# Four PSUM banks for a step's seven products, their sums on VectorE, relu, square and cast on ScalarE, the low part on GpSimd

## The chip, the cores and the metric

The kernel runs on one core of one Trainium2 chip. The time is device microseconds (us) of one execution; the figure quoted is the median of several runs. Engines: PE is TensorE (PEld its weight loads), DVE is VectorE, ACT is ScalarE, POOL is GpSimd, SP issues DMAs.

## What is computed

```python
X = np.fft.rfft(x, axis=1)                      # x: 8 x 3008 x 256
Yr = Xr @ w_r - Xi @ w_i + b_r
Yi = Xr @ w_i + Xi @ w_r + b_i
Y  = soft_threshold(Yr, 0.01) + 1j * soft_threshold(Yi, 0.01)
y  = np.fft.irfft(Y, n=3008, axis=1).reshape(24064, 256)
h  = y @ w_in                                   # 256 x 2048
out = (np.maximum(h, 0) ** 2) @ w_out           # 2048 x 256
```

All inputs are float32. Most products are made with numbers split in a high and a low part of type fp32r (a cast for the high part, a subtraction for the low one): high x high, high x low, low x high, three matmuls for one product.

## The kernel before

**The transform (called the first half here).** 3008 = 47 x 64, so a batch goes through four stages. `Fwd` is the 47-point part: per batch 13 pieces of 120 x 256, each loaded, folded by a sum and a difference (GpSimd), split, multiplied with `am_sb`, and stored to DRAM (`s1`). `Pair` takes two of 24 groups of bins: `fwd` (64-point part, plain float32, four matmuls), `sums` (a third operand), `mix` and `shrink` (the products with w_r and w_i, 18 matmuls, bias and soft threshold), `back` (six matmuls) and a store to `s3`. `Back` loads two rows of `s3`, splits them (`split`: ScalarE casts, GpSimd subtracts three times) and multiplies with `dx_sb` (`mm`); VectorE adds the two halves of the result into `yr`, which holds the columns of one token tile. Batch 0 goes through plain float32 twins of these (`Fwd32`, `Unit32`) in a front part, in which w_in and w_out are also unpacked from 64-bit floats.

**The second half.** The 48 token tiles (six for a batch, 500 or 504 tokens) go through 8 steps each, 384 steps in all. A step `Step(t, n)` makes 256 columns of `h` for its tile as a 2 x 2 block product with seven half-size products instead of eight (Strassen and Winograd): `Tokens.sums` and `split` make the seven operands of the tile (`yt0`, `yt1`, on GpSimd and ScalarE), `win_sums` those of w_in. Each of the seven is three matmuls of 250 or 252 columns (L474), 21 a step. `first` issues all seven into three PSUM banks `pa`, `pb`, `pc`, the last one (A12 x B21) into the half of `pa` that p1 was copied from: ScalarE copies p1, VectorE forms u2 (L488), v (L489) and the four quarters of `c` (L490, L493, L496). `second` makes relu and square: quarters 0 and 1 in one VectorE operation (L500), quarters 2 and 3 in two of ScalarE (L501, L502); then ScalarE casts all four to `mg0` and VectorE subtracts for the low part `mg1` (both in the helper `halves`, L84 and L88). `out(j)` is six matmuls of 500 or 504 columns with w_out into two accumulators `pso0` and `pso1` (L515), two `out` a step; after a tile's last step ScalarE copies the accumulators and they are stored.

**PSUM** has eight banks: two for `pso`, three in turn for the step's `psh`, three in turn for everything of the first half (`psf`).

**Order.** The program is written slot by slot: slot 2n holds `first` of step n and the second `out` of step n-2, slot 2n+1 `second` of step n and the first `out` of step n-1. The tasks of the first half for the next two batches are sorted by due slots (`pair_tasks`, `fwd_tasks`, `back_tasks`) and put between. A scheduler then sets the order of each engine's instructions, from its own estimate of times. Loads on SP's queue follow each other (`load_next`); constants for `Pair.back` (`kcm`) are loaded by GpSimd's queue. Each engine executes its instructions in the order given.

## Time and profile before

| | us |
|---|---|
| median of 3 runs | 2931.07 (2927.35 to 2939.08) |
| the profiled execution's own time | 2935.55 |
| its span, first to last instruction | 2933.8 |
| PE busy | 2681.6 (91%), 17038 matmuls |
| PEld busy | 2383.9 (81%) |
| DVE busy | 2262.4 (77%) |
| ACT busy | 1603.8 (55%) |
| POOL busy | 1696.1 (58%) |

The busy time of a pipelined matmul runs to its modelled end, while the next one has already started; so the distance between starts in the timeline tells what a matmul costs, and the idle time before a weight load tells what PE waited for. A wait for several semaphores is put down to the one that came last.

### The profile page before, as it was taken

To read this page: it belongs to the slowest core of one execution; us is meant where nothing else is said; L and a number is where in the kernel's file an instruction comes from. 1 tells how busy PE (TensorE), PEld (TensorE's weight loads), DVE (VectorE), ACT (ScalarE), POOL (GpSimd) and SP (SyncE) were. 2 spreads that over 40 slices of the span, in tenths; PEclk is the share of its full clock that TensorE was granted. 3 is DMA by queue.
4 is the path that set the end of the run, shared out by engine and by line. 5 is a ranking of instruction groups with operands and counts; after the bars stand their busy time and mean duration, and the time that the engine had idled before them with its cause. 6 is when DMAs were issued, how large, how long until landed. Compare 5 with 4: busy or idle time off the path is not lost.

```text
span 2933.8 us, 47287 instructions
## 1 busy us (share of the span) xinstructions
PE 2681.6 (91%) x17038; PEld 2383.9 (81%) x17038; DVE 2262.4 (77%) x3835; ACT 1603.8 (55%) x3147; POOL 1696.1 (58%) x1689
## 2 busy tenths in 40 slices
PE   5678988999999998999899998999999999999998
PEld 3567877888888887888788887888888888888787
DVE  5855877788888877788767887788877877877776
ACT  2455555555565565556455564556555555555554
POOL 1076776776767586576656765577766546433310
PEclk9889999999999999999999999999999999999999
DMA  8322232232222222122221221122221111100000
GB/s 238 126 62 88 84 89 72 73 87 74 74 70 80 66 82 77 42 77 82 64 63 58 74 83 56 56 69 77 79 69 51 57 47 54 42 16 28 16 15 15
DMA packets 139179, 200.35 MB, mean 68 GB/s; under 512 B 14611, under 2 KB 87683, under 8 KB 138947
## 3 DMA queue, kind: packets, MB, share of 16 engines
q1 hardware_dynamic: 126403, 174.49, 19.5%
q0 software_dynamic: 12544, 22.84, 3.3%
q8 instruction: 136, 2.23, 0.3%
q14 instruction: 96, 0.79, 0.1%
HBM read 121.91 MB, written 75.37 MB: 67 GB/s over the span
## 4 chain that ended last, share of the span: by engine, by line
PE 41%; DVE 24%; POOL 14%; ACT 7%; DMA 7%; issue 6%; SPq 0%; POOLq 0%; DVEq 0%; ACTq 0%
PE pso L515 19%; PE psh L474 13%; DVE mg L88 6%; PE psf L276 4%; POOL dul L88 3%; DMA du<-s 3%; DVE kv L298 3%; DVE mv L489 3%; DVE mc L500 2%; POOL duh L88 2%; ACT mg L84 2%; POOL yt L88 2%; POOL mc L88 2%; DVE mu L488 1%; POOL xs L204 1%
## 5 line engine op out<-in xcount | busy, mean ns | idle before, releaser
L515 PE MATMUL pso<-mg,wout 128*128 128x500 f32 (+1 forms) x4608 | 1219.1, 400 | 69.9 <-DVE mg L88 41.9
L474 PE MATMUL psh<-yt,win 128*128 128x250 f32 (+1 forms) x8064 | 1111.2, 283 | 53.4 <-DVE mu L488 28.0
L474 PEld LDWEIGHTS psh<-yt,win 128*128 128x128 f32 x8064 | 1047.3, 191 | 102.5 <-DVE mu L488 35.7
L515 PEld LDWEIGHTS pso<-mg,wout 128*128 128x128 f32 x4608 | 823.2, 191 | 248.7 <-DVE mg L88 88.6
L88 DVE TENSOR_TENSOR mg<-mc,mg 128x1000 fp32r<-128x1000 f32 (+1 forms) x384 | 549.8, 1432 | 202.4 <-ACT mg L84 201.3
L501 ACT ACTIVATE mc<-mc 128x500 f32<-128x500 f32 (+1 forms) x384 | 239.7, 624 | 414.7 <-DVE mc L493 414.0
L84 ACT CAST mg<-mc 128x1000 fp32r<-128x1000 f32 (+1 forms) x384 | 396.6, 1033 | 83.4 <-DVE mc L500 75.6
L500 DVE SCALAR_TENSOR_TENSOR mc<-mc 128x500 f32<-128x500 f32 (+1 forms) x384 | 363.5, 947 | 9.0
L489 DVE TENSOR_TENSOR mv<-psh,mu 128x500 f32<-128x500 f32 (+1 forms) x384 | 260.5, 678 | 46.4 <-PE psh L474 13.5
L88 POOL TENSOR_TENSOR duh<-du,duh 32x512 fp32r<-32x512 f32 x128 | 186.7, 1458 | 162.7 <-ACT duh L84 123.9
L493 DVE TENSOR_TENSOR mc<-psh,mv 128x500 f32<-128x500 f32 (+1 forms) x384 | 256.8, 669 | 0.7 <-PE psh L474 0.4
L488 DVE TENSOR_TENSOR mu<-psh,mp 128x250 f32<-128x250 f32 (+1 forms) x384 | 158.6, 413 | 125.1 <-ACT mp L84 123.3
L502 ACT ACTIVATE mc<-mc 128x500 f32<-128x500 f32 (+1 forms) x384 | 239.7, 624 | 7.6
L88 POOL TENSOR_TENSOR dul<-du,duh 64x256 fp32r<-64x256 f32 x256 | 227.5, 889 | 18.8
L88 POOL TENSOR_TENSOR xl<-xs,xh 120x256 fp32r<-120x256 f32 x182 | 166.0, 912 | 108.6 <-ACT xh L84 70.4
L496 DVE TENSOR_TENSOR mc<-psh,mp 128x250 f32<-128x250 f32 (+1 forms) x384 | 157.8, 411 | 89.6 <-PE psh L474 88.5
L276 PE MATMUL psf<-wx,kxh 128*128 128x256 f32 x1008 | 217.5, 286 | 5.7 <-DVE yr L436 3.1
L88 POOL TENSOR_TENSOR ksl<-kv,ksh 128x512 fp32r<-128x512 f32 x84 | 124.8, 1486 | 148.6 <-ACT ksh L84 147.1
L84 ACT COPY mp<-psh 128x250 f32<-128x250 f32 (+1 forms) x384 | 140.2, 365 | 109.0 <-PE psh L474 93.1
L88 POOL TENSOR_TENSOR mc<-yr 128x250 f32<-128x250 f32 (+1 forms) x96 | 72.0, 772 | 211.6 <-DVE mg L88 209.8
L204 POOL TENSOR_TENSOR xs<-xt 120x256 f32<-120x256 f32 x182 | 156.0, 857 | 51.8 <-DMA xt<-x_in 39.6
L276 PEld LDWEIGHTS psf<-wx,kxh 128*128 128x128 f32 x1008 | 171.4, 192 | 11.3 <-issue 2.9
(96 smaller groups left out, 3576.6 us busy)
## 6 DMA issues: line engine op xcount, KB each, us to landing
s<-ku SPq DMA_DIRECT2D x192, 128.0 KB, 1.8
du<-s SPq DMA_DIRECT2D x128, 192.0 KB, 2.7
s<-xe SPq DMA_DIRECT2D x92, 240.0 KB, 2.4
xt<-x_in SPq DMA_DIRECT2D x91, 240.0 KB, 3.2
kcm<-cm_in POOLq DMA_DIRECT2D x84, 256.0 KB, 3.3
ka<-s SPq DMA_DIRECT2D x84, 256.0 KB, 3.5
out<-mo SPq DMA_DIRECT2D x64, 250.0 KB, 2.1
kb<-bm_in SPq DMA_DIRECT2D x84, 128.0 KB, 2.1
```

Of the source, the lines that this page charges most:

```text
L84: return act.copy(out=out, in_=in_)
L88: return eng.tensor_tensor(out=out, in0=a, in1=b, op=ALU.subtract)
L204: return eng.tensor_tensor(out=out[:, :n], in0=self.xt[:, :n, 0], in1=self.xt[:, :n, 1], op=(ALU.add, ALU.subtract)[t])
L276: self.last = nc.tensor.matmul(ps, l, wx[j][:, k, c, :], start=n == 0, stop=n == 5)
L474: nc.tensor.matmul(ps, win[w][:, self.n, a], y[:, b], start=j == 0, stop=j == 2)
L488: dve.tensor_add(out=u2, in0=pa[:, 1], in1=p1)
L489: dve.tensor_tensor(out=v, in0=pb, in1=u2.unsqueeze(1).broadcast_to([128, 2, h]), op=ALU.add)
L493: dve.tensor_add(out=c[:, 1:3], in0=pc, in1=v)
L500: dve.scalar_tensor_tensor(out=c[:, 0:2], in0=c[:, 0:2], scalar=0.0, in1=c[:, 0:2], op0=ALU.max, op1=ALU.mult)
L501: act.activation(c[:, 2:4], c[:, 2:4], AF.Relu)
L502: act.activation(c[:, 2:4], c[:, 2:4], AF.Square)
L515: nc.tensor.matmul(acc[t][d][:, :2 * h], wout[w][:, f, dsl], self.g[g][:, j], start=f == 0 and k == 0, stop=f == NF - 1 and k == 2,)
```

## The change

Nine things are changed together.

1. A step has four banks of its own, one buffer each: `pa` (A11, S2), `pb` (S1, S3), `pc` (S4, A22), `pd` (A12); `psf` has two banks in the main part instead of three (six in the front part).
2. `first` issues four products, `second` the other three. p1 is copied by VectorE.
3. Relu, square and cast of all four quarters run on ScalarE as three operations of 1000 or 1008 columns; the subtraction for the low part runs on GpSimd. L500 and the VectorE subtraction are gone.
4. The slots are: 2n: `first` of n, first `out` of n-2; 2n+1: second `out` of n-2, then `second` of n.
5. `then` chains every matmul of the steps, and every operation of the steps on VectorE, ScalarE and GpSimd, in program order; the scheduler can only put work of the first half between.
6. `Fwd` is one float32 matmul each for sum and difference instead of three fp32r ones: no split, one ScalarE copy of 512 columns instead of two of 256, one bank instead of two.
7. The split of what `Back` reads is made before the store: `store_back` stores a high and a low part (two stores instead of one); the low part is a VectorE subtraction from PSUM, in the front part a GpSimd one. `Back` loads in three DMAs instead of one and multiplies at once.
8. In `Pair` the third operand is added by VectorE from PSUM and the bias likewise; two GpSimd sums, one more addition and a ScalarE copy are gone.
9. `Tokens` runs in smaller pieces (two `sums`, four `split`), `yr` has one buffer, and columns that belong to the next tile wait in `dy` and are copied by GpSimd (`put`). Due slots are new.

```diff
 MAIN = {
-    "xt": 1, "xs": 1, "xh": 1, "xl": 1, "xe": 1, "du": 1, "duh": 1, "dul": 1, "kv": 1, "kp": 1, "kq": 1, "ksh": 1,
-    "ksl": 1, "kxl": 1, "mo": 1, "mp": 1, "mu": 1, "mv": 1, "mc": 3, "kb": 1,
+    "xs": 1, "xe": 1, "du": 1, "kv": 1, "kp": 1, "kq": 1, "ksh": 1, "ksl": 1, "kxl": 1, "kb": 1, "yr": 1,
+    "ms": 1, "mp": 1, "mu": 1, "mv": 1, "mc": 3, "mo": 1,
 }
...
+        def run(self):
+            ps = bank([128, 2, D])
+            for t in range(2):
+                nc.tensor.matmul(ps[:M1, t], am32[:, t], self.u[:, t], start=True, stop=True)
+            self.ev = T("xe", [M1, 1, 2, D], F32)
+            copy(act, self.ev[:, 0], ps[:M1])
+            self.store()
+
+    def store_back(b, g, ps, eng):
+        uh = T("kuh", [128, D], F32R)
+        ul = T("kul", [128, D], F32R)
+        done = copy(act, uh, ps)
+        if eng is None:
+            sub(dve, ul, ps, uh)
+        else:
+            u = T("ku", [128, D], F32)
+            done = copy(act, u, ps)
+            sub(eng, ul, u, uh)
+        rows = s3[b].rearrange("m p c -> (m p) c")
+        for v, m in ((uh, 4 * g), (ul, 128 + 4 * g if 4 * g < 64 else 32 + 4 * g)):
+            nc.sync.dma_start(rows[m * NP:m * NP + 128], v.bitcast(F32))
+        return done
...
+    def then(eng, op, *args, **kwargs):
+        with tc.issue_after(last_of[eng].ins) if eng in last_of else nullcontext():
+            last_of[eng] = op(*args, **kwargs)
...
         def first(self):
-            pa, pb, pc = (ps_h.tile([128, 2, 256], F32, name="psh")[:, :, :h] for _ in range(3))
+            self.ps = pa, pb, pc, pd = [bank([128, 2, 256], f"psh{j}")[:, :, :h] for j in range(4)]
...
-            copy(act, p1, pa[:, 0])
-            dve.tensor_add(out=u2, in0=pa[:, 1], in1=p1)
...
+            then(dve, copy, dve, p1, pa[:, 0])
+            then(dve, dve.tensor_add, out=u2, in0=pa[:, 1], in1=p1)
+            then(dve, dve.tensor_add, out=v, in0=pb, in1=u2.unsqueeze(1).broadcast_to([128, 2, h]))
+            then(dve, dve.tensor_add, out=c[:, 3], in0=pb[:, 0], in1=v[:, 1])
+
+        def second(self):
+            h, c = self.h, self.c
+            pc, pd = self.ps[2:]
             self.product(pc[:, 0], S4, B22)
             self.product(pc[:, 1], A22, T4)
-            dve.tensor_add(out=c[:, 1:3], in0=pc, in1=v)
-
-            self.product(pa[:, 0], A12, B21)
-            dve.tensor_add(out=c[:, 0], in0=pa[:, 0], in1=p1)
-
-        def second(self):
-            h, c = self.h, self.c
-            dve.scalar_tensor_tensor(out=c[:, 0:2], in0=c[:, 0:2], scalar=0.0, in1=c[:, 0:2], op0=ALU.max, op1=ALU.mult)
-            act.activation(c[:, 2:4], c[:, 2:4], AF.Relu)
-            act.activation(c[:, 2:4], c[:, 2:4], AF.Square)
...
-            halves(self.g[0], self.g[1], c.rearrange("p (f j) h -> p f (j h)", f=2), dve)
+            self.product(pd[:, 0], A12, B21)
+            then(dve, dve.tensor_add, out=c[:, 1:3], in0=pc, in1=self.v)
+            then(dve, dve.tensor_add, out=c[:, 0], in0=pd[:, 0], in1=self.p1)
...
+            then(act, act.activation, c, c, AF.Relu)
+            then(act, act.activation, c, c, AF.Square)
+            then(act, copy, act, g[0], c)
+            then(pool, sub, pool, g[1], c, g[0])
...
         n, k = divmod(m, 2)
+        if k and 0 <= n - 2 < len(steps):
+            steps[n - 2].out(1)
         if n < len(steps):
             (steps[n].second if k else steps[n].first)()
-        if 0 <= n - 2 + k < len(steps):
-            steps[n - 2 + k].out(1 - k)
+        if not k and 0 <= n - 2 < len(steps):
+            steps[n - 2].out(0)
```

Three places show how the order moves. Names end in buffer numbers, which tie an operand to the instruction that made it; `x2` is two such instructions in a row.

PE, in the last tile, before: the last product of a step, then `out` of the step ahead of it (`mg0_33597` is made from `psh_33554`, the step before `psh_33607`).

```order
L474 MATMUL psh_33607<-yt0_33167,win0_90 128x250
L474 MATMUL psh_33607<-yt0_33167,win1_91 128x250
L474 MATMUL psh_33607<-yt1_33168,win0_90 128x250
L515 MATMUL pso0_33334<-mg0_33597,wout0_92 128x500
L515 MATMUL pso0_33334<-mg0_33597,wout1_93 128x500
L515 MATMUL pso1_33335<-mg0_33597,wout0_92 128x500
L515 MATMUL pso1_33335<-mg0_33597,wout1_93 128x500
L515 MATMUL pso0_33334<-mg1_33598,wout0_92 128x500
```

PE, the same place in the change: the fourth product of `first`, then `out` of the step two ahead (`mg0_32125` is made from `psh0_32078`; the steps `psh0_32131` and `psh0_32184` lie after it).

```order
L455 MATMUL psh1_32185<-yt0_31666,win0_81 128x250
L455 MATMUL psh1_32185<-yt0_31666,win1_82 128x250
L455 MATMUL psh1_32185<-yt1_31667,win0_81 128x250
L455 MATMUL pso0_31941<-mg0_32125,wout0_83 128x500
L455 MATMUL pso0_31941<-mg0_32125,wout1_84 128x500
L455 MATMUL pso0_31941<-mg1_32126,wout0_83 128x500
```

Between the last product of a step and the first use of its `mg1` there now stand 33 products and 14 matmuls of `out`; before there stood 21 and 16.

VectorE, one step in the last tile, before:

```order
L488 TENSOR_TENSOR mu_33611<-psh_33607,mp_33610 128x250
L489 TENSOR_TENSOR mv_33612<-psh_33608,mu_33611 128x500
L88 TENSOR_TENSOR mg1_33598<-mc_33560,mg0_33597 128x1000
L496 TENSOR_TENSOR mc_33613<-psh_33607,mp_33610 128x250
L490 TENSOR_TENSOR mc_33613<-psh_33608,mv_33612 128x250
L493 TENSOR_TENSOR mc_33613<-psh_33609,mv_33612 128x500
L500 SCALAR_TENSOR_TENSOR mc_33613<-mc_33613 128x500
```

And in the change:

```order
L89 COPY mp_32188<-psh0_32184 128x250
L455 TENSOR_TENSOR mu_32189<-psh0_32184,mp_32188 128x250
L455 TENSOR_TENSOR mv_32190<-psh1_32185,mu_32189 128x500
L455 TENSOR_TENSOR mc_32191<-psh1_32185,mv_32190 128x250
L455 TENSOR_TENSOR mc_32191<-psh2_32186,mv_32190 128x500
L455 TENSOR_TENSOR mc_32191<-psh3_32187,mp_32188 128x250
```

The two operations that read and write SBUF alone (L500 and the subtraction) are gone; the copy of p1 has come, and every operation left reads PSUM.

ScalarE in the middle of the program, two steps, before (`psf`, `kv`, `xs` are tiles of the first half):

```order
L501 ACTIVATE mc_14471<-mc_14471 128x504
L84 COPY ke_15498<-psf_15480 128x512
L502 ACTIVATE mc_14471<-mc_14471 128x504
L84 CAST mg0_14538<-mc_14471 128x1008
L84 COPY mp_14569<-psh_14566 128x252
L501 ACTIVATE mc_14572<-mc_14572 128x504
L84 CAST xh_15696<-xs_15695 120x256
L84 COPY xe_15427<-psf_15589 120x256
L502 ACTIVATE mc_14572<-mc_14572 128x504
L84 COPY mp_14687<-psh_14684 128x252
L84 CAST ksh_15579<-kv_15571 128x512
L84 CAST mg0_14624<-mc_14572 128x1008
```

ScalarE in the change, two steps in the middle of the program:

```order
L455 ACTIVATE mc_13675<-mc_13675 128x1008 x2
L88 CAST mg0_13715<-mc_13675 128x1008
L88 COPY kq_13729<-psf_13721 128x256
L88 CAST kxh_13726<-psf_13721 128x512
L455 ACTIVATE mc_13756<-mc_13756 128x1008
L88 COPY dy_13734<-psf_13735 128x188
L88 CAST kxh_13726<-kp_13728 128x256
L455 ACTIVATE mc_13756<-mc_13756 128x1008
L88 CAST ksh_13660<-kv_13652 128x512
L88 CAST mg0_13811<-mc_13756 128x1008
```

GpSimd over the same two steps in the change (before, no operation of a `Step` stood on this engine):

```order
L92 TENSOR_TENSOR mg1_13716<-mc_13675,mg0_13715 128x1008
L92 TENSOR_TENSOR kxl_13727<-kp_13728,kxh_13726 128x256
L92 TENSOR_TENSOR ms_13791<-yr_13436 128x252
L92 TENSOR_TENSOR ksl_13661<-kv_13652,ksh_13660 128x512
L92 TENSOR_TENSOR mg1_13812<-mc_13756,mg0_13811 128x1008
```

The step's three ScalarE operations stand in a fixed order with operations of the first half between them, and the subtraction for `mg1` stands among GpSimd's work of the first half.

## Rows read from the trace of the kernel before

**Rows 1.** The page, part 1: span and busy time of each engine.

```profile
span 2933.8 us, 47287 instructions
...
PE 2681.6 (91%) x17038; PEld 2383.9 (81%) x17038; DVE 2262.4 (77%) x3835; ACT 1603.8 (55%) x3147; POOL 1696.1 (58%) x1689
```

**Rows 2.** Timeline, PE, 2709 to 2714 us: start, us, engine, line, count.

```profile
2709.37 1.90 PE L474 MATMUL psh<-yt,win 128*128 128x252 f32 x15
...
2711.11 2.90 PE L515 MATMUL pso<-mg,wout 128*128 128x504 f32 x12
...
2713.84 2.27 PE L474 MATMUL psh<-yt,win 128*128 128x252 f32 x18
```

**Rows 3.** Timeline, one step near the end; in brackets idle before, and releaser.

```profile
2906.21 2.60 PE L474 MATMUL psh<-yt,win 128*128 128x250 f32 x21
...
2908.62 1.19 DVE L88 TENSOR_TENSOR mg<-mc,mg 128x1000 fp32r<-128x1000 f32 x1
...
2908.65 3.30 PE L515 MATMUL pso<-mg,wout 128*128 128x500 f32 x12
...
2909.87 1.67 PEld L515 LDWEIGHTS pso<-mg,wout 128*128 128x128 f32 x8 [0.57 <-DVE mg L88]
...
2911.79 2.60 PE L474 MATMUL psh<-yt,win 128*128 128x250 f32 x21
...
2912.95 1.03 ACT L84 CAST mg<-mc 128x1000 fp32r<-128x1000 f32 x1
...
2914.20 1.19 DVE L88 TENSOR_TENSOR mg<-mc,mg 128x1000 fp32r<-128x1000 f32 x1
```

**Rows 4.** Lines by form, PEld: busy us, mean ns, idle before (us), releasers.

```profile
L474 PEld LDWEIGHTS psh<-yt,win 128*128 128x128 f32 x8064 | 1047.3, 191 | 102.5 <-DVE mu L488 35.7 <-DVE mc L496 17.1 <-issue 6.3
...
L515 PEld LDWEIGHTS pso<-mg,wout 128*128 128x128 f32 x4608 | 823.2, 191 | 248.7 <-DVE mg L88 88.6 <-ACT mg L84 27.1 <-ACT mo L84 6.9
...
L224 PEld LDWEIGHTS psf<-xh,am_sb 120*120 120x120 f32 x364 | 59.0, 189 | 31.0 <-ACT xh L84 24.4 <-DVE yr L436 1.5 <-ACT ku L84 0.9
...
L224 PEld LDWEIGHTS psf<-xl,am_sb 120*120 120x120 f32 x182 | 33.8, 186 | 9.8 <-POOL xl L88 8.9
```

**Rows 5.** Lines by form, PE: products of `Fwd.half`, and float32 ones of `Unit32`.

```profile
L224 PE MATMUL psf<-xh,am_sb 120*120 120x256 f32 x364 | 79.1, 297 | 20.9 <-ACT xh L84 18.2 <-DVE yr L436 1.9 <-ACT ku L84 0.5
...
L224 PE MATMUL psf<-xl,am_sb 120*120 120x256 f32 x182 | 53.5, 294 | 6.4 <-POOL xl L88 6.0 <-DVE mc L493 0.3
...
L373 PE MATMUL psf<-w,kx 128*128 128x256 f32 x192 | 50.1, 407 | 1.4 <-ACT kx L366 1.0
```

**Rows 6.** Timeline near 130 us, PE, float32 products of 256 columns.

```profile
130.32 1.89 PE L373 MATMUL psf<-w,kx 128*128 128x256 f32 x8
```

**Rows 7.** Lines by form, VectorE, ScalarE, GpSimd, operations of the steps.

```profile
L88 DVE TENSOR_TENSOR mg<-mc,mg 128x1000 fp32r<-128x1000 f32 x256 | 365.2, 1427 | 121.8 <-ACT mg L84 121.2
...
L500 DVE SCALAR_TENSOR_TENSOR mc<-mc 128x500 f32<-128x500 f32 x256 | 238.1, 930 | 6.1
...
L489 DVE TENSOR_TENSOR mv<-psh,mu 128x500 f32<-128x500 f32 x256 | 173.3, 677 | 29.1 <-PE psh L474 7.1 <-DVE mu L488 1.4
...
L488 DVE TENSOR_TENSOR mu<-psh,mp 128x250 f32<-128x250 f32 x256 | 105.8, 413 | 104.9 <-ACT mp L84 103.7
...
L88 POOL TENSOR_TENSOR yt<-mc,yt 128x1000 fp32r<-128x1000 f32 x32 | 67.8, 2120 | 65.6 <-ACT yt L84 65.3
...
L88 POOL TENSOR_TENSOR yt<-mc,yt 128x1008 fp32r<-128x1008 f32 x16 | 41.3, 2579 | 20.2 <-ACT yt L84 20.0
```

**Rows 8.** Windows: us, PE, PEld, DVE, ACT, POOL busy, PEclk, DMA, GB/s.

```profile
60.00:130.00 70.00, 51.98 (x235) 42.25 (x236) 69.31 (x164) 32.98 (x81) 0.00 (x0) 0.95 0.48 152
...
300.00:2934.00 2634.00, 2465.23 (x15934) 2206.69 (x15933) 2076.28 (x3462) 1473.47 (x2858) 1571.40 (x1553) 0.98 0.21 62
```

**Rows 9.** Waits: who waited, for whom: us in total, times, longest us.

```profile
POOL ksl L88 <- ACT ksh L84: 147.1, 34, 13.8
...
ACT duh L84 <- DMA du<-s: 83.7, 53, 4.5
```

More of the change, by code (lines that the diff above doesn't have):

```diff
@@ L1 @@
-from contextlib import ExitStack
+from contextlib import ExitStack, nullcontext
 import numpy as np
@@ L510, in out @@
             if f == 0:
-                acc[t] = [ps_o.tile([128, 512], F32, name=f"pso{d}") for d in range(2)]
+                acc[t] = [bank([128, 512], f"pso{d}") for d in range(2)]
             for d in range(2):
@@ L543, in fwd_tasks @@
         for q in range(J):
-            f, at = Fwd(b, q), start + 2 * q * step
-            jobs += [(at, f.load), (at, lambda f=f: f.half(0)), (at + step, lambda f=f: f.half(1))]
+            f, at = Fwd(b, q), start + q * step
+            jobs += [(at - 2.5, f.load), (at - 0.8, f.add), (at + 0.3, f.run)]
         return jobs
```

235 lines of the change are left out of this document (118 added, 117 removed).

## The prediction, made before the changed kernel had run

> **What bounds the kernel now.** Read the page's busy times first: TensorE (PE) is busy 91% of 2933.8 us, VectorE 77%, GpSimd 58%, ScalarE 55% [rows 1]. No engine is full, so the next question is what a step costs when PE waits for nothing, and what it costs as it is. A dense piece of the timeline answers the first: 15 products take from 2709.37 to 2711.11 us, 0.116 us each, and 12 matmuls of `out` from 2711.11 to 2713.84, 0.2275 us each [rows 2]. A step is 21 and 12 of them: 2.44 + 2.73 = 5.17 us. In the last tiles, where no work of the first half is left, the steps start 5.58 us apart (2906.21 and 2911.79), so 0.41 us is lost in each, and the row in it names what for: the weight load of `out` waits for VectorE's subtraction [rows 3]. That subtraction (2908.62 to 2909.81) also stands ahead of the next step's sums, so VectorE is part of a loop that runs slower than PE.
>
> For the whole run I take the idle time ahead of the weight loads. For the products it is 102.5 us. For `out` it is 248.7 us, but a load (0.191 us) is shorter than a 0.2275 us matmul, and 4608 x 0.036 = 168 us of idle come from that alone; so I count only what has a named releaser: 88.6 + 27.1 + 6.9 = 122.6 us [rows 4]. Together the steps wait **225 us**. The two operations of VectorE that touch SBUF alone are also unsteady: the 1000-column subtraction has a mean of 1427 ns against 1.19 us in the quiet stretch [rows 3, 7], the 500-column relu and square 930 ns against 677 ns for a sum of the same width from PSUM [rows 7].
>
> **The change, part by part.** The sum is made against the profiled execution's own 2935.55 us, which is 4.5 us above the median of 2931.07.
>
> *Waits of the steps.* VectorE loses both operations that touch SBUF alone, (1427 + 930) ns a step, and gains a copy like L488's 413 ns; what is left is 4 x 0.413 + 2 x 0.677 = 3.0 us of a 5.17 us step. ScalarE has three operations of 1000 columns, priced as the cast's 1.03 us [rows 3]: 3.1 us. GpSimd has one subtraction, 2.12 us as for `yt` (2.58 at 1008 columns) [rows 7]. None of them can bound a pure step; the loop through VectorE is open. What has to fit now is the way from the last product of a step to the first use of its `mg1`. PE has 33 products and 14 matmuls of `out` to do meanwhile: 3.83 + 3.19 = 7.0 us. The way itself is the rest of the 0.68 us sum (0.33, as three products run beside it), 0.41, 3 x 1.03 and 2.12, 5.95 us (6.4 at 1008), plus four hand-overs. The longest in view is 0.22 us (cast ended 2913.98, subtraction began 2914.20 [rows 3]), and the others are shorter, so I take 0.5 us in all: 6.45 to 6.9 us. It fits by 0.1 to 0.6 us. In the stages with work of the first half the window is longer: counted in the order of instructions with the spacings above, half the steps have 9.0 us or more and one in ten under 7.7; ScalarE's other work between relu and cast adds 0.4 us in the middle case and over 1.3 in one of ten. So the 0.41 us per step go, 384 x 0.41 = 157 us, and the remaining 225 - 157 = 68 us, delays by other work in the queues, I leave standing. **-157 us**, bounds -225 (all gone) and 0 (new waits take their place); a price above zero is the second rival's.
>
> *`Fwd` in plain float32.* Removed are 546 products of 256 columns [rows 5], at the spacing above 256/252 x 0.116 = 0.118 us: 64.4 us. Added are 182 float32 matmuls, which the profile shows as two each: eight such took 1.89 us with 0.41 for the last, so 0.211 us apart [rows 5, 6]: 364 x 0.211 = 76.8. **+12 us**, on PE's own time. With the split goes what PE waited for: 31.0 + 9.8 us ahead of these loads [rows 4]. About 10 us I keep for the folds that now release PE directly: **-31 us**, bounds -41 and 0.
>
> *`Back` without a split.* The split's ScalarE cast and GpSimd subtractions go, hidden work today. But PE then waits for the load itself, and ScalarE waited 83.7 us in 53 places for it [rows 9]. The product is due 1.6 slots behind its load, where the split was due after 1.5, so a late load would show on PE. I take **0**, bounds -20 and +84. The extra DMAs (1283 issued on SP's queue for 835) lie beside a DMA share of 0.21 [rows 8].
>
> *Two `psf` banks for three.* In the order 32 of some 760 sums of the first half have less than 1.5 us of PE's work between the sum that held their bank and themselves, against 42 of some 850 before. A bank is freed by one copy behind at most a 1.03 us cast, so at worst 32 x 1.6 = 51 us. **+10 us**, bounds 0 and 51.
>
> *Clock.* From 300 us on the granted clock averages 0.98 [rows 8]; with levels of 2.4 and 1.2 GHz that costs 0.02 x 2634 = 53 us. Fewer waits should leave fewer falls, but weight loads run ahead of the matmuls, so part of the 225 us above never reached them, and I take only **-10 us**, bounds 0 and -40.
>
> *Both ends.* In the front part VectorE is busy 69.3 of 70 us [rows 8], and 24 GpSimd subtractions now run beside it. If each lengthens one of its operations as L500 is lengthened (930 - 677 ns), that is 6 us; I take +5. At the end the 6.45 us way lies behind one `out` pair (2.73) instead of a shorter way: +2. **+7 us**, bounds 0 and 15.
>
> GpSimd stays under the span even if nothing is taken off it: 1696.1 + 256 x 2.12 + 128 x 2.58 = 2569 us [rows 1, 7]. The smaller additions on VectorE and ScalarE fit in what those lose or have free.
>
> Sum: 2935.55 - 157 + 12 - 31 + 0 + 10 - 10 + 7 = 2766.5, and 4.5 less for the median: **2762 us**, 5.8% below before.
>
> **The rivals.**
>
> *1. Most waits stay.* If the waits come from the shared queues rather than the loop through VectorE, only a third of the 225 us goes, and the clock gives nothing: 2935.55 - 75 + 12 - 31 + 10 + 7 - 4.5 = 2854 us. For it: 0.1 to 0.6 us of room is thin, and a chain of three engines meets three queues. Against: the window is longer wherever the queues are fuller.
>
> *2. GpSimd holds the low part up: slower.* Its queue is in order, and today `ksl` waits there for ScalarE's `ksh` 147.1 us in 34 places, 4.3 us each [rows 9]. If each of the 84 pairs held the next `mg1` that long, with 1 us of it in the room, PE would lose 84 x 3.3 = 277 us: 2762 + 277 = 3039 us. The change loses from the point where a pair's hold takes all it saves, 169/84 = 2.0 us beyond the room, so from about 3 us. Against it: in the order shown, ScalarE's cast of `ksh` stands ahead of the very cast that `mg1` needs, so part of the hold is a wait that `mg1` has anyway. The Trainium skill (GPSIMD Engine Reference, sections 3 and 4.1) speaks against this move: elementwise work with two inputs belongs on VectorE, since GpSimd takes about twice as long. The trace agrees in direction, 2120 ns against 1427 and 1190 [rows 3, 7]; by that rule alone the outcome would be this rival.
>
> *3. Nearly dense.* If the unsteadiness of VectorE is what made the queues late, all 225 us go, the banks cost nothing and the clock gives 40: 2935.55 + 12 - 225 - 31 - 40 + 7 - 4.5 = 2654 us. For it: no step's VectorE operation is left that reads two SBUF tiles, and those from PSUM keep their 677 and 413 ns. The Trainium skill (SBUF — State Buffer, section "two separate sides") states why: VectorE with two SBUF inputs and GpSimd lock the same pair of ports against each other for a whole instruction. The 1427 and 930 ns [rows 7] agree, and by that rule the outcome leans to this rival. Against: the first half keeps its own waits, and ScalarE's queue is as mixed as before.
>
> *4. One wait for another.* The steps wait as long as before for something else, a tile's late operands or its accumulators: 2935.55 + 12 - 31 + 10 + 7 - 4.5 = 2929 us, no change.
>
> **How the numbers follow.** The forecast has 0.50, rival 1 0.20, rival 3 0.15, rival 4 0.06, rival 2 0.09. A change of 0.5%, 15 us, is about what can be told from none. Faster: 0.50 + 0.20 + 0.15 = 0.85; same 0.06; slower 0.09. The range reaches down to rival 3 (2650) and up past rival 1 with the two-bank bound added, 2854 + 41 = 2895, so 2900; outside lie rivals 2 and 4.
>
> **What would show it.** The last tiles' steps start 5.2 us apart; the waits of weight loads named after `mg` and `mu` fall from 225 to about 70 us; PE's waits for `xh` and `xl` are gone and float32 matmuls 0.21 us apart stand in their place; VectorE's step operations keep 413 and 677 ns; GpSimd's subtraction is near 2.1 us. Wrong would be: long waits of PE for GpSimd's `mg` (rival 2), for `du` loads, or for evacuations of `psf`; or last steps that still start 5.5 us apart.

## The result, and the profile after

| | before | after |
|---|---|---|
| median | 2932.42 us (4 runs, 2927.35 to 2939.08) | 2754.43 us (4 runs, 2750.85 to 2756.83) |
| profiled span | 2933.8 us | 2751.2 us |
| mean granted clock | 0.972 | 0.978 |

The change makes the kernel faster by 178 us: ratio 0.9391, 95% interval 0.9368 to 0.9413. The forecast was 2762 us. The page of the changed kernel, part 1, against [rows 1]:

```profile
span 2751.2 us, 47098 instructions
...
PE 2614.5 (95%) x16856; PEld 2362.4 (86%) x16856; DVE 1748.7 (64%) x3787; ACT 1663.6 (60%) x2434; POOL 1635.3 (59%) x1282
```

PE's busy share is 95%, VectorE's fell from 77 to 64%, and GpSimd stays below 60% although 912 us of low parts were put on it. The lines by form of PE's weight loads, as in [rows 4] (busy us, mean ns, idle before, releasers; in this kernel L455 is the line of every operation of a step, L228 the float32 products of `Fwd`, L432 the first products of `Back`):

```profile
L455 PEld LDWEIGHTS psh<-yt,win 128*128 128x128 f32 x8064 | 1035.0, 190 | 55.3 <-ACT yt L88 15.7 <-POOL yt L92 5.1
L455 PEld LDWEIGHTS pso<-mg,wout 128*128 128x128 f32 x4608 | 832.0, 190 | 170.2 <-POOL mg L92 21.7 <-ACT mo L88 7.5 <-ACT mg L88 0.7
...
L228 PEld LDWEIGHTS psf<-xs,am 120*120 120x120 f32 x364 | 57.9, 188 | 14.1 <-POOL xs L207 8.2 <-DVE yr L442 2.6
...
L432 PEld LDWEIGHTS psf<-dx_sb,du 128*128 128x128 f32 x256 | 49.5, 193 | 33.9 <-issue 20.6 <-ACT mg L88 2.9 <-DMA du<-s 2.6
```

Counted as the prediction counted, the steps wait 55.3 + 21.7 + 7.5 + 0.7 = 85 us, for 225 before [rows 4]. VectorE's u2 and `mg` are gone from the releasers. The operations of a step by form, as in [rows 7]:

```profile
L455 DVE TENSOR_TENSOR mv<-psh,mu 128x500 f32<-128x500 f32 x256 | 173.4, 678 | 24.5 <-PE psh L455 2.5 <-DVE mu L455 0.5
...
L455 DVE TENSOR_TENSOR mu<-psh,mp 128x250 f32<-128x250 f32 x256 | 106.8, 417 | 7.2
...
L89 DVE COPY mp<-psh 128x250 f32<-128x250 f32 x256 | 106.4, 415 | 32.2 <-PE psh L455 21.5
```

```profile
L92 POOL TENSOR_TENSOR mg<-mc,mg 128x1000 fp32r<-128x1000 f32 x256 | 605.2, 2364 | 394.4 <-ACT mg L88 393.6
L92 POOL TENSOR_TENSOR mg<-mc,mg 128x1008 fp32r<-128x1008 f32 x128 | 307.3, 2401 | 226.3 <-ACT mg L88 226.0
```

VectorE's sums from PSUM keep their time, 678 and 417 ns, with GpSimd at work beside them. GpSimd's subtraction takes 2364 and 2401 ns. The timeline of the last tile, where the steps run alone (PE, VectorE, ScalarE, GpSimd):

```profile
2719.59 2.62 PE L455 MATMUL psh<-yt,win 128*128 128x250 f32 x21
...
2724.81 2.61 PE L455 MATMUL psh<-yt,win 128*128 128x250 f32 x21
...
2725.71 0.68 DVE L455 TENSOR_TENSOR mc<-psh,mv 128x500 f32<-128x500 f32 x1 [1.93 <-PE psh L455]
...
2726.74 2.12 ACT L455 ACTIVATE mc<-mc 128x1000 f32<-128x1000 f32 x2 [2.00 <-DVE mc L455]
...
2728.93 1.03 ACT L88 CAST mg<-mc 128x1000 fp32r<-128x1000 f32 x1
...
2729.97 1.21 PE L455 MATMUL psh<-yt,win 128*128 128x250 f32 x9
...
2730.04 2.35 POOL L92 TENSOR_TENSOR mg<-mc,mg 128x1000 fp32r<-128x1000 f32 x1 [2.86 <-ACT mg L88]
```

The products of successive steps start 5.22 and 5.16 us apart, for 5.58 before [rows 3]. The first nine products of the 21 at 2724.81 end a step, near 2725.9; relu, square and cast follow at 2726.74 and 2728.93, and GpSimd is done at 2730.04 + 2.35 = 2732.39. That way of 6.5 us is the one that the prediction laid out (6.45 to 6.9 us, room for 7.0).

**An account of the span.** A weight load stands ahead of every matmul, so the loads' busy time and the idle time ahead of them add up to the span, less about 6 us. With the idle time split by what the load is for (sums over the groups of that view), the kernels that are compared below read, in us:

| kernel | loads busy | idle, products | idle, `out` | idle, first half | span | clock |
|---|---|---|---|---|---|---|
| before | 2383.9 | 102.5 | 248.7 | 192.7 | 2933.8 | 0.972 |
| engines and slots alone | 2407.5 | 119.5 | 166.7 | 218.2 | 2918.0 | 0.962 |
| four banks alone | 2371.7 | 85.0 | 174.7 | 204.3 | 2842.1 | 0.978 |
| after | 2362.4 | 55.3 | 170.2 | 157.1 | 2751.2 | 0.978 |
| after, no fixed order | 2349.9 | 71.0 | 123.3 | 136.2 | 2686.5 | 0.987 |
| the same, old `Back` | 2361.1 | 83.4 | 136.7 | 156.8 | 2744.1 | 0.980 |

Not all of the idle time is waiting: of the 170.2 us ahead of `out` after the change only 29.9 have a releaser among those listed above. From before to after the idle time ahead of the products gives 47 us, that ahead of `out` 78, that of the first half 36, and the loads' own time 21, together the 183 us of the span.

### The profile page after: what moved, and what is told of

It reads as the page before. It is cut to its first block, busy times and chain, and to the rows that moved or that the text cites. A ratio compares the mean times of both kernels' runs of the same rounds, so it can differ in the third digit from the quotient of the medians.

```text
span 2751.2 us, 47098 instructions
## 1 busy us (share of the span) xinstructions
PE 2614.5 (95%) x16856; PEld 2362.4 (86%) x16856; DVE 1748.7 (64%) x3787; ACT 1663.6 (60%) x2434; POOL 1635.3 (59%) x1282
## 4 chain that ended last, share of the span: by engine, by line
PE 75%; POOL 6%; DVE 5%; ACT 4%; issue 3%; DMA 2%; POOLq 0%; SPq 0%; DVEq 0%; ACTq 0%
PE pso L455 33%; PE psh L455 27%; PE psf L293 6%; POOL mg L92 2%; PE psf L228 2%; PE psf L325 2%; PE psf L272 2%; ACT mc L455 2%; DVE kv L314 1%; DVE mc L455 1%; DMA du<-s 1%; POOL xs L207 1%; POOL yt L92 1%; PE psf L436 1%; PE psf L435 1%
## 5 line engine op out<-in xcount | busy, mean ns | idle before, releaser
L92 POOL TENSOR_TENSOR mg<-mc,mg 128x1000 fp32r<-128x1000 f32 (+1 forms) x384 | 912.5, 2376 | 620.7 <-ACT mg L88 619.6
L455 PE MATMUL pso<-mg,wout 128*128 128x500 f32 (+1 forms) x4608 | 1167.3, 395 | 20.1 <-POOL mg L92 13.8
L455 PE MATMUL psh<-yt,win 128*128 128x250 f32 (+1 forms) x8064 | 1102.5, 283 | 14.3 <-ACT yt L88 12.5
L455 PEld LDWEIGHTS psh<-yt,win 128*128 128x128 f32 x8064 | 1035.0, 190 | 55.3 <-ACT yt L88 15.7
L455 ACT ACTIVATE mc<-mc 128x1000 f32<-128x1000 f32 (+1 forms) x768 | 802.6, 1045 | 374.9 <-DVE mc L455 365.5
L455 PEld LDWEIGHTS pso<-mg,wout 128*128 128x128 f32 x4608 | 832.0, 190 | 170.2 <-POOL mg L92 21.7
L455 DVE TENSOR_TENSOR mc<-psh,mv 128x500 f32<-128x500 f32 (+3 forms) x768 | 419.4, 548 | 573.3 <-PE psh L455 538.7
L455 DVE TENSOR_TENSOR mv<-psh,mu 128x500 f32<-128x500 f32 (+1 forms) x384 | 260.6, 679 | 37.5 <-PE psh L455 5.7
L89 DVE COPY mp<-psh 128x250 f32<-128x250 f32 (+1 forms) x384 | 159.7, 416 | 88.4 <-PE psh L455 72.1
L314 DVE TENSOR_TENSOR kv<-psf,ke 64x256 f32<-64x256 f32 x336 | 141.9, 422 | 58.0 <-PE psf L293 45.5
L455 DVE TENSOR_TENSOR mu<-psh,mp 128x250 f32<-128x250 f32 (+1 forms) x384 | 160.5, 418 | 11.1
L455 DVE TENSOR_TENSOR mc<-psh,mp 128x250 f32<-128x250 f32 (+1 forms) x384 | 157.3, 410 | 12.7 <-PE psh L455 10.7
L88 ACT COPY dy<-psf 128x188 f32<-128x188 f32 x256 | 76.2, 311 | 121.8 <-PE psf L436 121.4
L293 PE MATMUL psf<-wx,kxl 128*128 128x256 f32 x504 | 142.4, 283 | 2.2 <-DVE kxl L92 2.2
L88 ACT COPY xe<-psf 120x512 f32<-120x512 f32 (+1 forms) x98 | 56.8, 580 | 124.4 <-PE psf L228 104.9
L88 ACT CAST kuh<-psf 128x256 fp32r<-128x256 f32 x192 | 68.0, 373 | 98.4 <-PE psf L325 83.0
L92 POOL TENSOR_TENSOR yt<-yr,yt 128x250 fp32r<-128x250 f32 (+1 forms) x96 | 89.7, 937 | 61.8 <-ACT yt L88 61.8
```

The source lines that it names most:

```text
L88: return act.copy(out=out, in_=in_)
L89: return eng.tensor_copy(out=out, in_=in_)
L92: return eng.tensor_tensor(out=out, in0=a, in1=b, op=ALU.subtract)
L293: self.last = nc.tensor.matmul(ps, l, wx[j][:, k, c, :], start=n == 0, stop=n == 5)
L314: dve.tensor_add(out=v[64 * r:64 * r + 64, g], in0=ps[gs], in1=self.e[gs, r])
L455: last_of[eng] = op(*args, **kwargs)
```

## The experiments

All times are medians of several runs, each compared with runs of the kernel before on the same chip (its medians there: 2926 to 2931 us). The edits are against the changed kernel unless another is named.

### 1. The low part on VectorE

```diff
-            then(pool, sub, pool, g[1], c, g[0])
+            then(dve, sub, dve, g[1], c, g[0])
```

> The changed kernel, with the low part back on VectorE and all else as changed. Theory (the gain is the opened loop through VectorE: no operation of a step on it touches SBUF alone): VectorE's busy time rises by about 384 x 1.43 = 550 us to 2300, the subtraction's mean is again 1.35 to 1.45 us beside GpSimd's work, and at least half of the gain of 178 us is lost: 2840 to 2900 us. Rival (the gain is the longer room, 33 products and 14 matmuls between a step's last product and its mg1): the way to mg1 gets 1.1 us shorter (1.2 for 2.35 us), so nothing is lost: 2735 to 2770 us.

Measured: 3412.66 us, ratio 1.167 (1.1651 to 1.1689), slower than before and outside both ranges. The timeline near the end, VectorE and PE:

```profile
3351.98 0.97 PE L455 MATMUL psh<-yt,win 128*128 128x250 f32 x6 [1.36 <-DVE mu L455]
...
3357.31 1.20 DVE L92 TENSOR_TENSOR mg<-mc,mg 128x1000 fp32r<-128x1000 f32 x1 [3.24 <-ACT mg L88]
...
3359.35 0.97 PE L455 MATMUL psh<-yt,win 128*128 128x250 f32 x6 [1.29 <-DVE mu L455]
```

The subtraction itself takes 1.20 us, half of GpSimd's. But the fixed order puts it ahead of the next step's copy of p1, so VectorE stands 3.24 us for ScalarE's cast, and PE stands behind VectorE's u2. Steps start 7.37 us apart. What costs here is a place in an in-order queue, not the operation.

### 2. All old engines

p1 is copied by ScalarE, quarters 0 and 1 take one VectorE operation, the low part is on VectorE; order, banks, slots and first half as changed.

```diff
-            then(dve, copy, dve, p1, pa[:, 0])
+            then(act, copy, act, p1, pa[:, 0])
...
-            then(act, act.activation, c, c, AF.Relu)
-            then(act, act.activation, c, c, AF.Square)
+            then(
+                dve, dve.scalar_tensor_tensor, out=c[:, 0:2], in0=c[:, 0:2], scalar=0.0, in1=c[:, 0:2],
+                op0=ALU.max, op1=ALU.mult,
+            )
+            then(act, act.activation, c[:, 2:4], c[:, 2:4], AF.Relu)
+            then(act, act.activation, c[:, 2:4], c[:, 2:4], AF.Square)
...
-            then(pool, sub, pool, g[1], c, g[0])
+            then(dve, sub, dve, g[1], c, g[0])
```

> The changed kernel with all of the old engines for a step: p1 copied by ScalarE, quarters 0 and 1 by VectorE in one operation, 2 and 3 by ScalarE, low part by VectorE; order, banks and first half as changed. Theory (loop through VectorE): most of the gain of 178 us is gone, 2860 to 2930 us. Rival (room): the way is no longer than now, 2740 to 2780 us.

Measured: 2819.85 us, ratio 0.964 (0.9626 to 0.9654), between the ranges. In the fixed order the new engines are worth 65 us. PE's loads by form show where:

```profile
L455 PEld LDWEIGHTS psh<-yt,win 128*128 128x128 f32 x8064 | 1039.3, 189 | 142.5 <-DVE mu L455 51.4 <-PE psh L455 51.1 <-DVE mc L455 2.4
```

Idle time ahead of the products is 142.5 us for 55.3; 51.4 of it are put down to u2 again, and 51.1 to PE's own matmuls.

### 3. The old slots

```diff
-    for m in range(2 * len(steps) + 4):
+    for m in range(2 * len(steps) + 3):
...
-        if k and 0 <= n - 2 < len(steps):
-            steps[n - 2].out(1)
         if n < len(steps):
             (steps[n].second if k else steps[n].first)()
-        if not k and 0 <= n - 2 < len(steps):
-            steps[n - 2].out(0)
+        if 0 <= n - 2 + k < len(steps):
+            steps[n - 2 + k].out(1 - k)
```

> The changed kernel with the slots of before: second out of n-2 after first, first out of n-1 after second. Between a step's last product and the first use of its mg1 stand 21 products and 8 matmuls of out, 2.44 + 1.82 = 4.3 us, against a way of about 6.9 us. Theory and rival agree in sign. If the way is as long as worked out, PE waits 1 to 2.6 us a step: 384 x 1 to 384 x 2.6, 3130 to 3750 us. If the room does not matter (the waits of before were VectorE's unsteadiness alone): under 2820 us.

Measured: 2852.56 us, ratio 0.9753 (0.9739 to 0.9768), 98 us above the change, again between the ranges. The upper range rested on a miscount: by the slots of this run 14 matmuls of `out` (6 + 6 + 2), not 8, stand between a step's last product and its first use of `mg1`, so the room is 2.44 + 3.19 = 5.6 us against a way of 6.5. The last tiles show it; timeline of PE:

```profile
2785.55 1.21 PE L455 MATMUL psh<-yt,win 128*128 128x250 f32 x9
...
2787.41 1.18 PE L455 MATMUL pso<-mg,wout 128*128 128x500 f32 x4 [0.19 <-POOL mg L92]
...
2791.19 1.21 PE L455 MATMUL psh<-yt,win 128*128 128x250 f32 x9
```

The steps start 5.64 us apart there, about half a microsecond more than in the change; over the whole run it is 98 / 384 = 0.26 us a step. The predicted wait for the low part is there, 75.9 us for 21.7:

```profile
L455 PEld LDWEIGHTS pso<-mg,wout 128*128 128x128 f32 x4608 | 791.8, 190 | 192.8 <-POOL mg L92 75.9 <-ACT mo L88 14.5 <-ACT mg L88 9.2
```

But all idle time ahead of `out` grew by 23 us only. That of the first half grew by 86, from 157.1 to 242.9: where the scheduler has work of the first half to put between, PE's loads wait for that work's own casts and subtractions instead.

### 4. No fixed order

```diff
     def then(eng, op, *args, **kwargs):
-        with tc.issue_after(last_of[eng].ins) if eng in last_of else nullcontext():
-            last_of[eng] = op(*args, **kwargs)
+        op(*args, **kwargs)
```

> The changed kernel without the chaining of a step's instructions: the scheduler is free again to order them. Theory (engines and room): 2740 to 2790 us, no more than 1% lost. Rival (the fixed order is what pays): 2820 to 2900 us, with waits of PE for mg and yt like before.

Measured: **2688.85 us**, ratio 0.9193 (0.9179 to 0.9207), 65 us below the change and outside both ranges. PE's loads by form, then PE's timeline in the last tiles:

```profile
L454 PEld LDWEIGHTS psh<-yt,win 128*128 128x128 f32 x8064 | 1062.1, 190 | 71.0 <-ACT yt L88 6.6 <-POOL yt L92 5.5 <-issue 5.0
L454 PEld LDWEIGHTS pso<-mg,wout 128*128 128x128 f32 x4608 | 812.5, 189 | 123.3 <-POOL mg L92 4.9
```

```profile
2648.60 1.79 PE L454 MATMUL psh<-yt,win 128*128 128x250 f32 x14
2650.23 1.06 PE L454 MATMUL pso<-mg,wout 128*128 128x500 f32 x4
2651.12 0.98 PE L454 MATMUL psh<-yt,win 128*128 128x250 f32 x7
2651.94 2.02 PE L454 MATMUL pso<-mg,wout 128*128 128x500 f32 x8
2653.79 0.86 PE L454 MATMUL psh<-yt,win 128*128 128x250 f32 x6
```

`out` waits 4.9 us for GpSimd's `mg` instead of 21.7. PE takes products and `out` in pieces, here of 4 to 14, as the scheduler estimated them to be ready, where the fixed order has blocks of 9, 12 and 21. By the account, `out` stands 47 us less than in the change, the first half 21 less, the products 16 more, and the loads take 13 less. In the fixed order a late piece stops PE; the changed kernel's timeline, ScalarE and PE, shows it at a change of tiles:

```profile
2705.81 0.57 ACT L88 COPY mo<-pso 128x500 f32<-128x500 f32 x1 [3.26 <-DMA out<-mo]
...
2706.44 2.32 PE L455 MATMUL pso<-mg,wout 128*128 128x500 f32 x9 [1.04 <-ACT mo L88]
...
2712.02 2.57 PE L455 MATMUL pso<-mg,wout 128*128 128x500 f32 x10 [0.36 <-POOL mg L92]
```

ScalarE's copy of an accumulator waits 3.26 us for the DMA of the one before, the relu behind it is late, and PE stands twice, for the copy and then for `mg`.

### 5. Engines and slots on the kernel before

The edits of runs 2 and 3 made the other way on the kernel before: p1's copy, relu and square, and the low part move as in the change, and the new slots are used. Banks, first half and the scheduler's order are the old ones.

```diff
-            copy(act, p1, pa[:, 0])
+            copy(dve, p1, pa[:, 0])
...
-            halves(self.g[0], self.g[1], c.rearrange("p (f j) h -> p f (j h)", f=2), dve)
+            halves(self.g[0], self.g[1], c.rearrange("p (f j) h -> p f (j h)", f=2), pool)
```

> The kernel before with two parts of the change only: the engines (p1 copied by VectorE, relu, square and cast of all four quarters on ScalarE, low part on GpSimd) and the new slots. Three psh banks in turn, the old first half, no fixed order. Theory A (engines and slots together take the step's waits away, the banks and the first half are worth little, and the scheduler is free as in the run without the fixed order, which took 2688.85): 2690 to 2740 us. Theory B (with three banks, and all seven products issued at once, the products of the next step wait for the sums on VectorE, and the fourth bank is what lets the new slots work): 2790 to 2860 us.

Measured: 2914.86 us, ratio 0.9948 (0.9933 to 0.9963), so these two parts, on which the prediction's largest term rested, are worth 16 us alone. Both theories fall. In the account, `out` waits 82 us less, but products, first half and loads take 66 us more, and the clock falls to 0.962. The page, part 1, and PE's loads by form:

```profile
PE 2669.3 (91%) x17038; PEld 2407.5 (83%) x17038; DVE 1653.4 (57%) x3451; ACT 1804.0 (62%) x2763; POOL 2349.1 (81%) x2073
```

```profile
L309 PEld LDWEIGHTS psf<-ksh,kcm 128*128 128x128 f32 x336 | 56.4, 207 | 48.7 <-ACT ksh L84 44.7 <-issue 0.3 <-DVE yr L436 0.3
```

ScalarE and GpSimd now carry the step's work and the whole old first half, and one operand of `Pair.back`, cast by ScalarE, holds PE up for 44.7 us, where it was 12.3 before. Where no work of the first half is left, the move does help: PE's timeline has steps of 5.19 us in the last tiles, for 5.58 in [rows 3], although a few others still stand behind u2 or c0.

```profile
2847.13 1.56 PE L474 MATMUL psh<-yt,win 128*128 128x250 f32 x12
...
2852.32 1.55 PE L474 MATMUL psh<-yt,win 128*128 128x250 f32 x12
```


### 6. Three step banks

A12 x B21 goes into the half of `pa` that p1 was copied from; the fixed order stays.

```diff
-            self.ps = pa, pb, pc, pd = [bank([128, 2, 256], f"psh{j}")[:, :, :h] for j in range(4)]
+            self.ps = pa, pb, pc = [bank([128, 2, 256], f"psh{j}")[:, :, :h] for j in range(3)]
...
-            pc, pd = self.ps[2:]
+            pd, _, pc = self.ps
...
-bufs={**MAIN, "psf": 2},
+bufs={**MAIN, "psf": 3},
```

> The changed kernel with three step banks instead of four: the last product A12 x B21 goes into the half of pa that p1 was copied from; psf gets the third bank back. In the fixed order `first` of the next step follows the last product directly and writes pa, which the sum c0 on VectorE still reads. Theory A (that wait is real): each step pays the sum of 0.68 us and the one of 0.41 us and their starts, 1.0 to 1.4 us, 384 times: 3140 to 3290 us. Theory B (banks are a convenience; the third psf bank gives a little back): 2735 to 2765 us.

Measured: 2865.97 us, ratio 0.9777 (0.9759 to 0.9796), 112 us above the change. The wait that Theory A names is there; timeline of PE:

```profile
2795.13 1.66 PE L455 MATMUL psh<-yt,win 128*128 128x250 f32 x12 [0.75 <-DVE mc L455]
...
2801.35 1.67 PE L455 MATMUL psh<-yt,win 128*128 128x250 f32 x12 [0.75 <-DVE mc L455]
```

Each pure step stands 0.75 us for the sum that reads the bank, and the steps are 6.22 us apart, 1.0 more than in the change. Over the whole run it is 112 / 384 = 0.29 us a step; where there is work of the first half, the scheduler can put some between.

### 7. No fixed order, low part on VectorE

Edits 1 and 4 together.

> The changed kernel without the fixed order of the steps (that run took 2688.85 us), and with the low part subtracted on VectorE instead of GpSimd. Theory A (the 3412.66 us of the run with the low part on VectorE came from the fixed order, in which VectorE stood behind ScalarE's cast; a scheduler that is free puts other VectorE work first): 2700 to 2790 us, steps 5.2 to 5.6 us apart in the last tile. Theory B (VectorE and its turn on SBUF with GpSimd are what is short, whatever the order): above 2850 us.

Measured: 2687.63 us, ratio 0.9171 (0.9154 to 0.9189), the same as run 4 (2688.85). VectorE is then busy 78% and GpSimd 30%:

```profile
PE 2585.1 (96%) x16856; PEld 2350.6 (88%) x16856; DVE 2103.4 (78%) x4171; ACT 1674.2 (62%) x2434; POOL 811.6 (30%) x898
```

So which engine makes the low part does not matter in this free order, and the 658 us of run 1 come only with the fixed one. The Trainium skill (GPSIMD Engine Reference, sections 3 and 4.1) would leave elementwise work on VectorE. Its reason, the slower GpSimd, agrees with 2364 ns against 1242 ns here; its consequence for the time depends on the order: following it costs 658 us in run 1 and nothing in this one.

### 8. Only PE's order fixed

```diff
-        with tc.issue_after(last_of[eng].ins) if eng in last_of else nullcontext():
+        with tc.issue_after(last_of[eng].ins) if eng is pe and eng in last_of else nullcontext():
```

> The changed kernel with the fixed order kept for the matmuls of the steps alone; VectorE, ScalarE and GpSimd are left to the scheduler. All engines fixed took 2754.43 us, none 2688.85. Theory A (what the fixed order costs is the matmuls' own order: PE stands behind a late operand although other products are ready): 2740 to 2765 us. Theory B (it is the order on VectorE, ScalarE and GpSimd, where a step's operation that is not ready yet holds up the next one and the first half's): 2685 to 2715 us.

Measured: 2758.87 us, ratio 0.9408 (0.9385 to 0.943), as with all engines fixed (2754.43). Fixing the matmuls' order alone brings the 65 us back (Theory A).

### 9. Four banks on the kernel before

```diff
-    ps_h = ctx.enter_context(tc.tile_pool(name="ps_h", bufs=3, space=PSUM))
-    ps_f = ctx.enter_context(tc.tile_pool(name="ps_f", bufs=3, space=PSUM))
+    ps_h = ctx.enter_context(tc.tile_pool(name="ps_h", bufs=4, space=PSUM))
+    ps_f = ctx.enter_context(tc.tile_pool(name="ps_f", bufs=2, space=PSUM))
...
-            pa, pb, pc = (ps_h.tile([128, 2, 256], F32, name="psh")[:, :, :h] for _ in range(3))
+            pa, pb, pc, pd = (ps_h.tile([128, 2, 256], F32, name="psh")[:, :, :h] for _ in range(4))
...
-            self.product(pa[:, 0], A12, B21)
-            dve.tensor_add(out=c[:, 0], in0=pa[:, 0], in1=p1)
+            self.product(pd[:, 0], A12, B21)
+            dve.tensor_add(out=c[:, 0], in0=pd[:, 0], in1=p1)
```

> The kernel before with the banks of the change alone: four psh banks, each for the same products in every step, A12 x B21 into the fourth, two psf banks instead of three. Engines, slots and first half as before, no fixed order. Engines and slots together were worth only 16 us here (2914.86). Theory A (what the step waits for is a bank that VectorE has not read yet, so the fourth bank carries the gain): 2770 to 2850 us, and the 88.6 us that PE waited after VectorE's u2 shrink below 40. Theory B (the gain hangs on the lighter first half, whose splits keep ScalarE, GpSimd and VectorE busy, and two psf banks cost the old first half something): 2900 to 2960 us.

Measured: 2853.44 us, ratio 0.9731 (0.9713 to 0.975), 76 us below the kernel before, though a bank was taken from the first half. PE's loads by form, against [rows 4]:

```profile
L474 PEld LDWEIGHTS psh<-yt,win 128*128 128x128 f32 x8064 | 1056.8, 191 | 85.0 <-ACT yt L84 17.5 <-DVE mu L488 10.5 <-DVE mc L496 4.8
L515 PEld LDWEIGHTS pso<-mg,wout 128*128 128x128 f32 x4608 | 810.8, 189 | 174.7 <-ACT mg L84 27.5 <-DVE mg L88 23.9 <-ACT mo L84 7.3
```

With the same engines, the wait named after VectorE's `mg` falls from 88.6 to 23.9 us and the one after u2 from 35.7 to 10.5. (The 88.6 us of the expectation are those after `mg`, not u2.) Theory A's time is 3 us too low at its upper end; its cause holds: much of what stood there under VectorE's name was due to a bank. The scheduler also chose another order of the matmuls with it (in the last tiles pieces of 2 to 15, for the blocks of 21 and 12 in [rows 3]), so this run does not separate the wait for a bank from the order; run 6, where the order is fixed, shows the wait by itself.

### 10. No fixed order, three step banks

Edits 4 and 6 together.

> The changed kernel without the fixed order and with three step banks instead of four (psf gets the third back): new engines, slots and first half, banks as before. With four banks this took 2688.85 us, and the same engines and slots with the old first half and three banks 2914.86; the 226 us between are split here. Theory A (banks): 2840 to 2900 us, PE waiting for the sum c0 on VectorE. Theory B (first half): 2690 to 2760 us, because a free scheduler puts `out` between the last product and the next step.

Measured: 2750.85 us, ratio 0.9389 (0.9375 to 0.9403). That is Theory B's range, but the fourth bank is worth 62 us here, so both count. Against run 5, which has the same engines, slots and number of banks, the new first half is worth 2914.86 - 2750.85 = 164 us.

### 11. No fixed order, old engines and slots

Edits 2, 3 and 4 together: of the change only the four banks, issued in two halves, and the new first half are left.

> The changed kernel without the fixed order, and with the old engines (p1 copied by ScalarE, quarters 0 and 1 in one VectorE operation, low part on VectorE) and the old slots: only the four banks and the new first half of the change are left. Theory A (without a fixed order engines and slots are worth next to nothing: their gains of 65 and 98 us in the runs with the fixed order are repairs of what that order does): 2685 to 2725 us. Theory B (they shorten the way to the low part whatever the order): 2750 to 2850 us.

Measured: 2705.49 us, ratio 0.9234 (0.9219 to 0.925), 17 us above run 4 and 49 below the whole change. Theory A holds. PE's timeline in the last tiles:

```profile
2651.72 2.59 PE L454 MATMUL psh<-yt,win 128*128 128x250 f32 x21
2654.15 2.90 PE L454 MATMUL pso<-mg,wout 128*128 128x500 f32 x12
2656.88 2.59 PE L454 MATMUL psh<-yt,win 128*128 128x250 f32 x21
```

These are the blocks of [rows 3], 21 products and 12 matmuls of `out`, with all of VectorE's old operations, and yet the steps start 5.16 us apart instead of 5.58: VectorE's work does not bound a pure step that has a fourth bank.

### 12. No fixed order, old `Back`

Edit 4, and `store_back` and `Back` as before the change.

```diff
+        def split(self):
+            self.uh = T("duh", [128, 2, D], F32R)
+            self.ul = T("dul", [128, D], F32R)
+            copy(act, self.uh[:M2], self.u)
+            sub(pool, self.uh[M2:], self.u[64:M2], self.uh[64:M2])
+            for p in range(2):
+                sub(pool, self.ul[64 * p:64 * p + 64], self.u[:64, p], self.uh[:64, p])
...
-            jobs += [(at, k.load), (at + 1.6, k.mm)]
+            jobs += [(at - 0.6, k.load), (at + 0.8, k.split), (at + 1.6, k.mm)]
```

> The changed kernel without the fixed order, with one part of the first half undone: what `Back` reads is split after the load as before (a ScalarE cast and three GpSimd subtractions, 0.62, 1.46 and twice 0.89 us in the kernel before), stored once and loaded in one DMA. Without the undoing 2688.85 us; the old first half as a whole costs about 150 us (2853.44 with four banks and the old first half, 2705.49 with the new one, both with the old engines and slots). Theory A (the term of the prediction: moving the split is worth nothing, the waits of `Back`'s matmuls are of the same size either way, 31.4 us before against 33.9 after): 2680 to 2705 us. Theory B (the 414 us that these subtractions put back on GpSimd, beside the 912 us of the step's low part, make `Back`'s operands and the low parts late): 2720 to 2780 us, GpSimd busy above 2000 us, PE's waits after GpSimd's mg and the subtraction of du together above 30 us.

Measured: 2748.62 us, ratio 0.9377 (0.9362 to 0.9393): 60 us above run 4. Theory B's time holds. Its details do not, though they point its way: the lines by form show what GpSimd does more,

```profile
L92 POOL TENSOR_TENSOR dul<-du,duh 64x256 fp32r<-64x256 f32 x256 | 188.6, 737 | 19.1
L92 POOL TENSOR_TENSOR duh<-du,duh 32x512 fp32r<-32x512 f32 x128 | 165.0, 1289 | 138.5 <-ACT duh L88 87.2 <-issue 39.3 <-POOL yt L92 2.6
```

354 us, less than the 414 expected; GpSimd is busy 1951 us, not above 2000, and PE's waits for `mg` and the split together are 5.8 + 13.0 + 1.8 = 20.6 us, not above 30. The cost does not stand in one wait, and the split, the single store and load and the due slots went back together. By the account against run 4, products wait 12 us more, `out` 13, the first half 21, and the loads take 11 more, with the clock at 0.980 for 0.987.

## Why the prediction was right, and where it was not

**The total was right, 2762 for 2754.43, but most of its cause was not, and that it came out so near is luck.** Four runs make a ladder, each rung one part of the change (the kernel before read 2926 to 2932 us beside them): kernel before 2929.28; four banks 2853.44 (-76); new first half, with the split issue of the seven products, 2705.49 (-148); new engines and slots 2688.85 (-17); fixed order 2754.43 (+66). In the same split the forecast had +10 for the banks, -19 for the first half (+12, -31 and 0), -157 for the waits that engines and slots were to end, and nothing for the order: errors of 66 to 140 us that cancel. The parts are not independent. With three banks the first half gives 164, and in the fixed order the engines give 65 and the slots 98.

*Waits of the steps, -157: right in size, wrong in cause.* They fell from 225 to 85 us, -140. The way of 6.5 us, the room of 7.0 and last steps 5.2 us apart were right, as were the prices from PSUM and ScalarE's 1031 and 1042 ns; GpSimd's 2.12 and 2.58 us were 2.36 and 2.40. The step that failed is "the loop through VectorE". The row named VectorE's `mg` as what `out` waited for, and the prediction inferred that the 0.41 us a step would go with VectorE's work, 384 times. Run 11 has all of that work back on VectorE, and its last steps are as dense as the change's; run 7 has the low part back and is as fast as run 4. Moving the work opens the last tiles too, as run 5 shows without a fourth bank, and `out` then stands 82 us less; but over the whole run other idle time takes 66 of them back, and 16 us are gained in all. Run 9 leaves the work where it was and adds a bank: it gains 76 us, and the named waits fall by 90. Whether engines and slots would gain more with three banks and a lighter GpSimd (81% busy in run 5) was not run.

*Two `psf` banks, +10: the wrong sign for the exchange.* The prediction priced the bank that the first half lost and gave the bank that the steps won nothing. Its worth was 62 to 76 us in a free order and 112 in the fixed one. The profile had hints: products waited behind u2 and c0, 35.7 and 17.1 us [rows 4], and both read banks that the next products write.

*`Back` without a split, 0 between -20 and +84: outside its bounds.* Run 12 puts it at -60 us, on the kernel without the fixed order. The prediction called the split hidden work, and set against its loss only PE's new wait for loads. That wait is there but small: this is the top of the list of PE's waits in the changed kernel,

```profile
PE psf L432 <- DMA du<-s: 19.8, 10, 7.2
...
PE pso L455 <- POOL mg L92: 13.8, 22, 1.7
```

19.8 us in 10 places. What the spread of run 12's cost suggests, though no run separates it from the stores and loads, is that the 414 us of subtractions and 79 us of casts stood in the queues in which steps, `Pair` and `Fwd` had their own operations; "hidden" held for PE, not for what stood behind them. The rest of the first half's 148 us was not taken apart: `Fwd`, the sums that left GpSimd for VectorE, smaller `Tokens` pieces and due slots came together in every run.

*`Fwd` in float32, +12 and -31: its rows came out as costed; alone it was not run.* The waits ahead of its loads went from 40.8 us to 14.1, -27, and those of the whole first half from 193 to 157. The records of the float32 matmuls, two for each, start as far apart as expected: here are four, the last of 0.38 us,

```profile
1506.00 1.03 PE L228 MATMUL psf<-xs,am 120*120 120x256 f32 x4
```

(1.03 - 0.38) / 3 = 0.217 us.

*Clock, -10: too small.* The mean granted clock leaves (1 - 0.972) x 2933.8 = 82 us unused before and (1 - 0.978) x 2751.2 = 61 after, so up to 21 us came from it. From 300 us on the windows give 0.99 where [rows 8] had 0.98:

```profile
300.00:2751.00 2451.00, 2381.88 (x15625) 2164.74 (x15624) 1565.19 (x3390) 1521.47 (x2168) 1489.20 (x1161) 0.99 0.29 84
```

Run 4 leaves 35 us unused, run 12 leaves 55 and run 5 111; but run 2 has a mean of 0.989 with a span of 2817.6 us, so fewer waits and a higher clock do not always go together.

*Both ends, +7: the tail about as expected.* It was put at +2; at the end PE stands three times, 2.7 us in all, of which 2.5 are for GpSimd's `mg`, where before it stood once, 1.53 us for ScalarE's cast:

```profile
2737.59 2.53 PE L455 MATMUL pso<-mg,wout 128*128 128x500 f32 x10 [0.74 <-POOL mg L92]
...
2742.84 2.58 PE L455 MATMUL pso<-mg,wout 128*128 128x500 f32 x10 [1.73 <-POOL mg L92]
```

In the front part VectorE is busy 68.9 us between 60 and 130 us, for 69.3 before [rows 8]; what the GpSimd work beside it costs was not separated.

*The fixed order, costed at nothing: +65 us.* The prediction used it to count the room and did not ask what it takes away. Run 8 shows that fixing the order of the matmuls is enough to cost it.

*The rivals.* GpSimd did not hold the low part up by 3 us a pair; `out` waited for `mg` 21.7 us in all. Rival 1 had the right suspicion, that much of the waiting comes from shared queues, but drew the wrong conclusion, since the change also emptied those queues. Rival 3 was wrong for the changed kernel. Run 4 comes within 35 us of its 2654, with the fixed order gone, but not by the cause that the rival names: run 7 has VectorE's subtraction of two SBUF tiles back and is as fast.
